# Linear attention and a gated mixture of four attention experts on one core: the work as a task graph with a list scheduler, and squares read from SBUF

## The chip, the core and the metric

The kernel runs on one core of a Trainium2 chip. The core has TensorE for matrix products (PE in the profile; its weight loads are PEld), VectorE (DVE), ScalarE (ACT), GpSimd (POOL), and SyncE (SP), which here only issues DMA transfers. Products land in PSUM, and DVE or ACT copy them from there to SBUF. The metric is the device time of one execution in microseconds (us), as the median of several runs. All inputs and outputs lie in HBM.

## The reference

The numbers are 8 batches, 8 heads, 576 tokens, 64 channels a head, 4 experts. Cut to what matters:

```python
kv = einsum('bhsd,bhse->bhde', k, v)              # 64x64 for each head
out = einsum('bhsd,bhde->bhse', q, kv)
rms = sqrt(mean(out * out, axis=-1) + 1e-06)
x = out / rms * g_norm                            # (8, 576, 512): the 8 heads side by side

logits = x @ w_gate                               # 4 experts, the best 2 kept, softmax of those two
for e in range(4):
    q, k, v = x @ wq[e], x @ wk[e], x @ wv[e]     # 512 -> 64
    scores = causal(scale * (q @ k.T))            # 576x576
    a = exp(scores - scores.max()) / sum
    out += weight_of(e) * (a @ v @ wo[e])         # 64 -> 512
```

## The kernel before

A batch has 576 tokens, which are cut into five blocks (four of 128, one of 64). The work on a batch is three Python generators.

`stage_a` is the linear attention. `kv_pair` multiplies k by v for two heads (80 small matmuls a batch, tile p_kv), and `kv_copy` copies the result twice: DVE into kvx, the operand of the next product, and ACT into a block diagonal tile kv2. `q_block` transposes q on PE (p_q), and DVE copies that to qT. kv2 is transposed (p_kt, kvT) and multiplied by the gate weights (p_kg), which adds four gate columns to each head of kvx. Then each of the five blocks is multiplied by kvx (p_out). DVE copies p_out to o_sb, ACT writes the squares of p_out to sq, and DVE sums sq into ms. When all five are there, a chain of eleven small DVE operations computes one over the root for all tokens (tiles half, u, w, y), and POOL multiplies o_sb by it into x_tok.

`stage_x` transposes x_tok on PE (p_x), and ACT copies it to xT.

`stage_s` is the experts. DVE computes the gates. `v_proj` makes v of all four experts, `proj` makes q and k of one pair of experts (p_proj; ACT copies it to qTp and kT). `scores` makes the scores in five pieces for each pair. A matmul there reads the 64 partitions of one expert of the pair, in kT and in qTp. ACT writes the exponential of each piece to PT, and POOL masks the diagonal. `pv` multiplies by v (p_O), DVE scales by gate over sum (inv, osc), `o_t` transposes (p_OT, OT). `final` multiplies by wo (p_y); ACT copies p_y to y, and SP stores y.

PSUM is two rings. "big" has three slots of two banks (p_out, p_proj, p_sc, p_O), "small" has two slots of one bank (p_kv, p_q, p_kt, p_kg, p_x, p_v, p_OT, p_y).

The order comes from two layers. `merge` interleaves the generators by the costs that they yield, so that in one turn `stage_s` of batch b runs beside `stage_x` of b + 1 and `stage_a` of b + 2. Within `stage_s` a string fixes the order of its parts:

```python
"Q0 Q0 V V S0 V S0 V S0 V S0 Q1 S0 Q1 S1 Y S1 Y S1 P0 P0 P0 S1 P0 P0 S1 Y T0 Y Y P1 P1 P1 P1 P1 T1"
```

The tile layer below then reorders the instructions by its own priorities, and can cut a part in two. Each engine runs its own list in order. Loads are issued by SP in the order in which they are written: batch 0, the weights, batches 1 and 2, then one batch for each turn.

Of the kernel before, what the change touches and what calls it, by code (L numbers as in the profile page):

```python
# [14 lines left out]
AX_X = mybir.AxisListType.X  # L15


@with_exitstack
def kernel(
# [45 lines left out]
    def small(shape, name, dtype=FP32):
        return ps1.tile(shape, dtype, tag="small", name=name)
# [6 lines left out]
    kr, vr, kvx, kv2s, sqs, lg8s, kTs, vexts, mss = [], [], [], [], [], [], [], [], []  # L73
    for j in range(2):
# [16 lines left out]
        nc.gpsimd.memset(t[:], 1.0)  # L91
        vexts.append(t)
        t = const.tile([P, NB, H], FP32, name=f"ms{j}")
        nc.gpsimd.memset(t[REM:P, NF], 1.0)
        mss.append(t)
    ob = const.tile([P, NB, H, GW], FP32, name="o_sb")
    nc.gpsimd.memset(ob[REM:P, NF], 0.0)
    for j in range(3):
        t = const.tile([P, H, Dh + 1], FP32, name=f"sq{j}")
        nc.gpsimd.memset(t[:, :, Dh : Dh + 1], 1e-6)  # L100
        sqs.append(t)
# [36 lines left out]

    loads = {0: load_qkv(0, fine=True)}

    g_wide = const.tile([P, 1], FP32, name="g_wide")
    for r in range(P // Dh):
        nc.sync.dma_start(g_wide[r * Dh : (r + 1) * Dh, :], g_norm.unsqueeze(1))
    wg_st = const.tile([P, NCH, E], FP32, name="wg_st")
    nc.sync.dma_start(wg_st[:], moe_w_gate.rearrange("(c p) e -> p c e", p=P))
    wg_bd = const.tile([P, NCH, 2, E], FP32, name="wg_bd")
    nc.gpsimd.memset(wg_bd[:], 0.0)
    for hh in range(2):
        pp = slice(hh * Dh, (hh + 1) * Dh)
# [3 lines left out]
    w_r = {}
    for name, wdram in (("v", moe_wv), ("q", moe_wq), ("k", moe_wk)):
        wr = const.tile([P, NCH, E, Hd], FP32R, name=f"w{name}_r")
        wf = wst.tile([P, NCH, E, Hd], FP32, name="w_stage", tag="w_stage")
        for e in range(E):
            nc.sync.dma_start(wf[:, :, e, :], wdram[e].rearrange("(c p) f -> p c f", p=P))
        nc.vector.tensor_scalar_mul(
            out=wr[:].rearrange("p c e f -> p (c e f)"),  # L160
            in0=wf[:].rearrange("p c e f -> p (c e f)"),
            scalar1=g_wide[:],
        )
        w_r[name] = wr
    loads[1] = load_qkv(1)
    wo_st = wst.tile([P, EP, D], FP32, name="wo_st", tag="w_stage")
    for pr in range(EP):
        nc.sync.dma_start(
            wo_st[:, pr, :], moe_wo[2 * pr : 2 * pr + 2].rearrange("two d m -> (two d) m")
        )  # L170
    wo_b = const.tile([P, EP, D], BF16, name="wo_b")
    nc.vector.tensor_copy(out=wo_b[:], in_=wo_st[:])

    def kv_pair(p_kv, c, kb, vb, krem, vrem):
# [9 lines left out]
    def kv_copy(p_kv, kvb, kv2):
        for hh in range(2):
            pp = slice(hh * Dh, (hh + 1) * Dh)
            nc.vector.tensor_copy(out=kvb[pp, :, hh, 0:Dh], in_=p_kv[pp, :, :])
            nc.scalar.copy(kv2[pp, :, hh * Dh : (hh + 1) * Dh], p_kv[pp, :, :])  # L188


    def stage_a(b, res):
        qb, kb, vb = loads[b]
        qT = s1.tile([P, NCH, S], FP32, tag="qT", name="qT", bufs=1)
        kvb, kv2 = kvx[b % 2], kv2s[b % 2]

        def q_block(i):
            t0, nt = blocks[i]
            p_q = small([P, NCH, P], "p_q")
            for c in range(NCH):
# [341 lines left out]
    for _ in y_gen:  # L541
        pass
# [30 lines left out]
```

## Time and profile before

| | |
|---|---|
| median of 3 runs | 328.1 us (324.1 to 328.66) |
| the profiled execution's own time | 324.47 us |
| span of its instructions | 322.5 us |
| granted TensorE clock, mean | 0.945 of full speed |
| PE busy | 276.0 us, 86% |
| PEld busy (weight loads) | 220.4 us, 68% |
| DVE busy | 189.2 us, 59% |
| ACT busy | 153.0 us, 47% |
| POOL busy | 79.5 us, 25% |
| chain that ended last | PE 70%, DVE 10%, ACT 9%, SP's queue 4% |

"Busy" of PE is a union of matmuls whose ends are modelled, and matmuls are pipelined: the next starts before the one ahead has drained. So the pace of PE is read from start to start within a group of equal instructions, and not from the length of one. The weight load of a matmul is an instruction of its own, shown on PEld.

### The profile page before, as it was taken

How to read it: one execution, taken by the hardware profiler on the slowest of the kernel's cores; microseconds unless marked ns; L12 is line 12 of the kernel's file. 1: busy time of each engine (PE TensorE's matmuls, PEld its weight loads, DVE VectorE, ACT ScalarE, POOL GpSimd, SP SyncE). 2: the span in 40 equal slices, each digit the busy share in tenths (PEclk: the TensorE clock that was granted, in tenths of full speed). 3: DMA queues.
4: the chain of work that ended last, by engine and by line, in shares of the span. 5: the costliest groups of instructions: out<-in, count | busy, mean ns of one | idle time of the engine just before them, and what ended most of it. 6: DMA issues, size and time to landing. Idle time of an engine off the chain costs nothing.

```text
span 322.5 us, 6704 instructions
## 1 busy us (share of the span) xinstructions
PE 276.0 (86%) x2624; PEld 220.4 (68%) x2624; DVE 189.2 (59%) x537; ACT 153.0 (47%) x273; POOL 79.5 (25%) x148
## 2 busy tenths in 40 slices
PE   1675579799979997999889996999889996999984
PEld 1565468588858775887667875887667875867641
DVE  0249948846884568646775578546774578424130
ACT  0203123653464654545554554545555554585843
POOL 8100600441044110702053101612052101630210
PEclk9959599999999999799999999799999999899977
DMA  6977999999704269194608372001200120021124
GB/s 195 243 199 195 205 301 223 298 180 276 152 2 133 64 202 192 41 253 127 169 3 269 81 182 58 2 0 67 82 2 2 65 83 0 0 100 53 65 83 147
DMA packets 75280, 40.30 MB, mean 125 GB/s; under 512 B 54000, under 2 KB 70384, under 8 KB 75248
## 3 DMA queue, kind: packets, MB, share of 16 engines
q1 hardware_dynamic: 75248, 39.86, 47.1%
q8 instruction: 21, 0.34, 0.5%
q14 instruction: 11, 0.09, 0.1%
HBM read 30.42 MB, written 9.44 MB: 124 GB/s over the span
## 4 chain that ended last, share of the span: by engine, by line
PE 70%; DVE 10%; ACT 9%; SPq 4%; issue 3%; POOL 1%; DMA 1%; DVEq 0%; ACTq 0%; POOLq 0%
PE p_proj L373 11%; PE p_out L242 11%; PE p_v L355 7%; PE p_sc L400 7%; PE p_O L451 7%; PE p_y L506 6%; PE p_q L200 6%; PE p_x L313 6%; PE p_kv L179 5%; ACT PT L410 3%; PE p_kg L224 3%; DVE o_sb L249 3%; SPq L134 2%; PE p_OT L484 2%; POOL x_tok L297 1%
## 5 line engine op out<-in xcount | busy, mean ns | idle before, releaser
L415 POOL TENSOR_SCALAR_AFFINE_SELECT PT<-PT 128x256 bf16<-128x256 bf16 (+1 forms) x80 | 29.3, 381 | 143.4 <-ACT PT L410 143.4
L410 ACT ACTIVATE PT<-p_sc 128x576 bf16<-128x576 f32 (+3 forms) x80 | 53.9, 714 | 20.1 <-PE p_sc L400 18.1
L297 POOL TENSOR_TENSOR x_tok<-o_sb,y 128x512 f32<-128x512 f32 (+1 forms) x40 | 42.0, 1080 | 85.1 <-DVE y L280 85.0
L242 PE MATMUL p_out<-kvx,qT 128*128 128x136 f32 (+1 forms) x320 | 48.1, 292 | 0.0
L400 PE MATMUL p_sc<-qTp,kT 64*128 64x288 f32 (+2 forms) x192 | 35.7, 358 | 10.7 <-ACT PT L410 5.9
L242 PEld LDWEIGHTS p_out<-kvx,qT 128*128 128x128 f32 (+1 forms) x320 | 40.2, 181 | 4.8 <-ACT sq L253 2.1
L253 ACT ACTIVATE sq<-p_out 128x512 f32<-128x512 f32 (+1 forms) x40 | 23.8, 596 | 39.9 <-DVE o_sb L249 38.4
L318 ACT CAST xT<-p_x 128x512 fp32r<-128x512 f32 (+1 forms) x40 | 21.8, 545 | 34.3 <-PE p_x L313 34.3
L400 PEld LDWEIGHTS p_sc<-qTp,kT 64*128 64x128 f32 x192 | 19.8, 185 | 21.9 <-ACT PT L410 8.5
L179 PE MATMUL p_kv<-v_b,k_b 128*64 128x64 f32 x512 | 25.7, 260 | 10.3 <-DMA v_b<-in_v_dram 10.3
L249 DVE COPY o_sb<-p_out 128x544 f32<-128x544 f32 (+1 forms) x40 | 28.7, 719 | 7.7 <-PE p_out L242 7.2
L362 DVE CAST vext<-p_v 128x256 bf16<-128x256 f32 (+1 forms) x40 | 17.0, 425 | 26.3 <-PE p_v L355 25.6
L259 DVE TENSOR_REDUCE ms<-sq 128x8 f32<-128x520 f32 (+1 forms) x40 | 27.4, 688 | 7.9 <-ACT sq L253 7.8
L205 DVE COPY qT<-p_q 128x512 f32<-128x512 f32 (+1 forms) x40 | 24.7, 634 | 11.6 <-PE p_q L200 11.0
L451 PEld LDWEIGHTS <-PT 128*128 128x128 bf16 (+2 forms) x480 | 24.1, 103 | 10.8 <-issue 5.3
L179 PEld LDWEIGHTS p_kv<-v_b,k_b 128*64 128x64 f32 x512 | 23.0, 173 | 12.2 <-DMA k_b<-in_k_dram 6.7
L451 PE MATMUL p_O<-vext,PT 128*128 128x65 bf16 (+2 forms) x480 | 30.3, 199 | 0.4 <-ACT PT L410 0.4
L313 PE MATMUL p_x<-ident_f,x_tok 128*128 128x128 f32 (+1 forms) x160 | 25.9, 289 | 5.4 <-POOL x_tok L297 4.3
L355 PE MATMUL p_v<-wv_r,xT 128*128 128x256 f32 (+1 forms) x160 | 28.3, 300 | 0.7 <-ACT kv L188 0.7
L373 PE MATMUL p_proj<-xT,wk_r 128*128 128x288 f32 x128 | 24.3, 314 | 3.6 <-ACT qTp L384 3.6
L506 PE MATMUL p_y<-wo_b,OT 128*128 128x512 bf16 (+1 forms) x80 | 25.1, 417 | 0.7 <-ACT OT L489 0.7
L511 ACT COPY y<-p_y 128x512 f32<-128x512 f32 (+1 forms) x40 | 23.0, 595 | 5.0 <-PE p_y L506 2.7
(67 smaller groups left out, 360.9 us busy)
## 6 DMA issues: line engine op xcount, KB each, us to landing
q_b<-in_q_dram SPq DMA_DIRECT2D x32, 256.0 KB, 5.2
out_dram<-y SPq DMA_DIRECT2D x32, 256.0 KB, 2.1
k_b<-in_k_dram SPq DMA_DIRECT2D x7, 1024.0 KB, 6.0
v_b<-in_v_dram SPq DMA_DIRECT2D x7, 1024.0 KB, 10.2
k_b<-in_k_dram SPq DMA_DIRECT2D x4, 256.0 KB, 4.7
v_b<-in_v_dram SPq DMA_DIRECT2D x4, 256.0 KB, 4.9
k_rem<-in_k_dram SPq DMA_DIRECT2D x8, 128.0 KB, 9.2
v_rem<-in_v_dram SPq DMA_DIRECT2D x8, 128.0 KB, 7.5
```

What stands on the lines that cost most here:

```text
L179: nc.tensor.matmul(p_kv[hh * Dh : (hh + 1) * Dh, c, :], lhsT=lk, rhs=rv, start=(j == 0), stop=(j == NF), skip_group_check=True,)
L242: nc.tensor.matmul(p_o[:nt, c // 2, (c % 2) * 2 * GW : (c % 2 + 1) * 2 * GW], lhsT=qT[:, c, t0 : t0 + nt], rhs=kvb[:, c, :, :].rearrange(" ...
L249: nc.vector.tensor_copy(out=ob[:nt, i].rearrange("p (k h) g -> p k (h g)", k=2), in_=p_o[:nt, :, 0 : 4 * GW])
L297: nc.gpsimd.tensor_tensor(out=xt[:nt], in0=ob[:nt, i, :, 0:Dh], in1=y[:nt, i * H : (i + 1) * H].unsqueeze(2).to_broadcast([nt, H, Dh]), op ...
L313: nc.tensor.transpose(p_x[:, c, :nt], xts[i][:nt, 2 * c : 2 * c + 2, :].rearrange("p h d -> p (h d)"), ident_f[:nt, :nt],)
L355: nc.tensor.matmul(p_v[:nt, :], lhsT=xT[:, c, t0 : t0 + nt], rhs=w_r["v"][:, c, :, :].rearrange("p e f -> p (e f)"), start=(c == 0), stop= ...
L373: nc.tensor.matmul(p_p[:, s, 0:HALF], lhsT=w_r[nm][:, c, 2 * pr : 2 * pr + 2, :].rearrange("p e f -> p (e f)"), rhs=xT[:, c, s * HALF : (s ...
L400: nc.tensor.matmul(p_s[:, el, o : o + hi - lo], lhsT=kTp[pb, kb * P : (kb + 1) * P], rhs=qTp[pb, lo:hi], start=True, stop=True,)
L410: nc.scalar.activation(PT[:, :, d0 : d0 + o], p_s[:, :, 0:o], ACTF.Exp, scale=scale)
L415: nc.gpsimd.affine_select(out=d, in_=d, compare_op=AluOpType.is_ge, fill=0.0, base=0, pattern=[[0, 2], [1, w]], channel_multiplier=-1,)
L451: nc.tensor.matmul(p_O[:nq, bank, (2 * n + el) * (Hd + 1) : (2 * n + el + 1) * (Hd + 1)], lhsT=PT[:nk, el, col : col + nq], rhs=vx[:nk, kb ...
L506: nc.tensor.matmul(p_y[:nq, :], lhsT=OT[:, pr, s0 : s0 + nq], rhs=wo_b[:, pr, :], start=(pr == 0), stop=(pr == EP - 1),)
```

## The change

The generators, `merge` and the string are gone. `graph` writes each piece of work as a task, with its engine, how long it holds the engine, when its result is there, the tasks that it needs, and the ring slots that it uses. `plan` is a list scheduler that runs when the program is built: again and again it takes the task that can start earliest, and of those of that engine that can start within 0.02 us of it the one of lowest `urgency`, a number for each kind of task from the tables OFFSET and STEP and the batch number. The kernel then emits the tasks in that order, under `manual_schedule`, in which the tile layer doesn't reorder. Tasks of equal urgency (the four parts of a load, blocks of the same q) come in the order in which Python walks a set, which the text doesn't fix: two builds of it stand in different orders at such places.

Beside the order, some operations are others:
- the squares are read from o_sb, so that p_out has one reader, the copy by DVE;
- the ACT copy of p_kv is one instruction for all partitions (kvc), without the block diagonal; p_kt takes two transposes instead of four, p_kg two matmuls instead of four, with gate weights laid out for that;
- kT is now two tiles for each pair, one for each expert, with zeros in the other expert's 64 partitions. A score matmul reads all 128 partitions, and the copy of k is two ACT instructions of 64 partitions;
- k and v come in two transfers each (four in batch 0), the gate weights are loaded first, and the weights wq, wk and wv behind k and v of batch 2.

The sizes of the two rings stay: `"sm": 2, "bg": 3`.

```diff
+    def pe(name, hold, needs, tiles=()):
+        add(name, "PE", hold, hold + 0.27, needs, tiles)
+
+    def act(name, took, needs, tiles=()):
+        add(name, "ACT", took - 0.10, took + 0.06, needs, tiles)
...
+        for c in R4:
+            piece = c if b == 0 else c // 2
+            pe(("kv", b, c), 0.88, [("lk", b, piece), ("lv", b, piece), ("lr", b)], (("sm", "kv", b), ("k", b), ("v", b)))
...
+            pe(("out", b, i), 0.93, [("qc", b, i), ("kvx", b), ("kgc", b)], (("bg", "out", b, i), ("qT", b)))
+            dve(
+                ("oc", b, i), 0.73, [("out", b, i), ("xm", b - 1, i), ("gl", b - 1), ("sq", b - 1, i)],
+                (("bg", "out", b, i),),
+            )
+            n = NB * b + i - 3
+            act(("sq", b, i), 0.60, [("oc", b, i), ("red", n // NB, n % NB)])
...
+    o = n[1] * PERIOD + OFFSET[kind]
+    if kind in STEP:
+        o += n[2] * STEP[kind]
...
+    while len(order) < len(tasks):
+        starts = []
+        for eng, ns in cand.items():
+            f = free[eng]
+            for n in ns:
+                t = ready[n]
+                for tl in tasks[n][4]:
+                    if tl not in held:
+                        t = max(t, min(slots[tl[0]], default=none))
+                if eng == "PE" and t > f - 0.15:
+                    t += 0.1
+                starts.append((max(t, f), prio[n], eng, n))
+        t0, _, eng, _ = min(starts)
+        t, _, _, n = min(((t, p, e, n) for t, p, e, n in starts if e == eng and t <= t0 + 0.02), key=lambda x: x[1])
...
-            sq = sqs[i % 3]
-            nc.scalar.activation(
-                sq[:nt, :, 0:Dh].rearrange("p (k h) d -> p k h d", k=2),
-                p_o[:nt, :, 0 : 4 * GW].rearrange("p k (h g) -> p k h g", g=GW)[:, :, :, 0:Dh],
-                ACTF.Square,
-                scale=1.0 / (Dh**0.5),
-            )
...
+    def sq_act(b, i):
+        nt = blocks[i][1]
+        nc.scalar.activation(
+            sqs[(NB * b + i) % 3][:nt, :, 0:Dh], ob[:nt, i, :, 0:Dh], ACTF.Square, scale=1.0 / (Dh**0.5)
+        )
...
+    def kvc_copy(b):
+        nc.scalar.copy(kvcs[b % 2][:], small(None, "kv", b)[:])
...
+    def k_proj_copy(b, pr):
+        for el in range(2):
+            pb = slice(el * Hd, (el + 1) * Hd)
+            nc.scalar.copy(
+                kTs[pr][el][pb, 0:S].rearrange("p (s n) -> p s n", s=2), big("k", b, pr)[pb, :, 0:HALF]
+            )
...
-                        pb = slice(el * Hd, (el + 1) * Hd)
-                        nc.tensor.matmul(
-                            p_s[:, el, o : o + hi - lo],
-                            lhsT=kTp[pb, kb * P : (kb + 1) * P],
-                            rhs=qTp[pb, lo:hi],
...
+                nc.tensor.matmul(
+                    p_s[:, el, o : o + hi - lo],
+                    lhsT=kTs[pr][el][:, kb * P : (kb + 1) * P],
+                    rhs=tiles["qTp", b, pr][:, lo:hi],
...
+    tasks = graph(B)
+    with tc.manual_schedule():
+        for _, _, n in plan(tasks, POOLS, {n: urgency(n) for n in tasks})[0]:
+            emit[n[0]](*n[1:])
```

The first place is on PE, where the second pair of experts of a batch in the middle gets its scores. Before, the end of the product p_proj for k, the last transposes p_OT of the batch ahead, and the score pieces p_sc stand in a row, and then come p_x and p_kv of other batches:

```order
L373 MATMUL p_proj<-xT,wk_r 128x288 x5
L484 LDWEIGHTS osc
L484 MATMUL p_OT<-ident_b,osc 128x128
L400 MATMUL p_sc<-qTp,kT_132 128x288
L484 LDWEIGHTS osc
L484 MATMUL p_OT<-ident_b,osc 128x64
L400 MATMUL p_sc<-qTp,kT_132 128x288 x3
L400 MATMUL p_sc<-qTp,kT_132 128x448 x2
L400 MATMUL p_sc<-qTp,kT_132 128x320 x2
L313 MATMUL p_x<-ident_f,x_tok 128x128 x4
L179 MATMUL p_kv<-v_b,k_b 64x64 x8
```

Now (p_k and p_q at L633 are the products for k and q, p_q at L433 transposes q of a later batch, kT_118 and kT_121 belong to the two experts):

```order
L633 MATMUL p_k<-xT,wk_r 128x288 x8
L633 MATMUL p_q<-xT,wq_r 128x288 x8
L448 MATMUL p_kt<-ident_f,kvc_80 128x128 x2
L433 MATMUL p_q<-ident_f,q_b 128x128 x4
L458 MATMUL p_kg<-wg_bd,kvT 128x16 x2
L659 MATMUL p_sc<-qTp,kT_118 128x288
L659 MATMUL p_sc<-qTp,kT_121 128x288
L433 MATMUL p_q<-ident_f,q_b 128x128 x4
L659 MATMUL p_sc<-qTp,kT_118 128x288
L659 MATMUL p_sc<-qTp,kT_121 128x288
L433 MATMUL p_q<-ident_f,q_b 128x64 x4
L659 MATMUL p_sc<-qTp,kT_118 128x448
```

Work of a later batch has moved between the product for k and the scores that need its copy, and between one score piece and the next.

The second place is SP's queue at the start. Before, the weights (w_stage) stand between the loads of batch 1:

```order
L134 DMA q_b<-in_q_dram 64x8x64
L143 DMA g_wide<-in_g_norm_dram 64x1 x2
L145 DMA wg_st<-in_moe_w_gate_dram 128x4x4
L158 DMA w_stage<-in_moe_wv_dram 128x4x64 x4
L116 DMA k_b<-in_k_dram 128x8x256
L158 DMA w_stage<-in_moe_wq_dram 128x4x64 x4
L116 DMA v_b<-in_v_dram 128x8x256
L158 DMA w_stage<-in_moe_wk_dram 128x4x64 x4
```

Now k and v of batch 2 are ahead of them:

```order
L369 DMA q_b<-in_q_dram 128x8x64 x4
L369 DMA q_b<-in_q_dram 64x8x64
L352 DMA v_b<-in_v_dram 128x4x256
L352 DMA k_b<-in_k_dram 128x4x256
L352 DMA v_b<-in_v_dram 128x4x256
L365 DMA k_rem_74<-in_k_dram 64x8x64
L365 DMA v_rem_76<-in_v_dram 64x8x64
L352 DMA k_b<-in_k_dram 128x4x256
L392 DMA w_stage<-in_moe_wq_dram 128x4x64 x4
L392 DMA w_stage<-in_moe_wk_dram 128x4x64 x4
```

The weights for q and k have moved behind batch 1 and behind k and v of batch 2.

## Rows read from the trace of the kernel before

**Rows 1.** Stretches: length, busy PE, PEld, DVE, ACT, POOL (instructions), clock, DMA share, GB/s

```profile
0.00:55.50 55.50, 34.75 (x325) 30.14 (x325) 29.74 (x67) 10.37 (x19) 14.07 (x33) 0.85 0.93 223
...
158.70:172.30 13.60, 11.03 (x148) 9.07 (x148) 10.67 (x38) 6.81 (x13) 6.29 (x8) 1.00 0.23 56
172.30:194.20 21.90, 21.52 (x180) 17.20 (x180) 12.67 (x30) 11.97 (x22) 2.51 (x7) 1.00 0.64 183
...
314.00:322.50 8.50, 3.93 (x9) 0.94 (x9) 0.00 (x0) 3.15 (x6) 0.00 (x0) 0.74 0.40 140
```

**Rows 2.** Chain that ended last, in order of time: start, length, what

```profile
55.54 1.26 PE p_proj L373 x8
...
158.69 1.34 PE p_proj L373 x8
...
165.16 2.01 ACT PT L410 x3
...
168.39 0.98 DVE gt L341
...
172.36 0.74 PE p_v L355 x4
...
194.21 1.34 PE p_proj L373 x8
```

**Rows 3.** Waits of PE's weight loads, 158.7 to 194.2 us: total, times, longest

```profile
PEld p_sc L400 <- ACT PT L410: 1.2, 1, 1.2
PEld p_proj L373 <- ACT qTp L384: 1.0, 1, 1.0
PEld p_sc L400 <- ACT kT L384: 1.0, 2, 0.8
PEld L451 <- issue: 0.6, 2, 0.4
...
PEld p_out L242 <- issue: 0.2, 1, 0.2
```

**Rows 4.** Groups of PE and PEld in the timeline (the first from the chain)

```profile
95.41 2.48 PE p_kv L179 x80
...
194.20 1.09 PEld L373 LDWEIGHTS p_proj<-xT,wq_r 128*128 128x128 f32 x8 [0.58 <-ACT sq L253]
196.77 1.08 PEld L451 LDWEIGHTS <-PT 128*128 128x128 bf16 x18
199.69 0.40 PE L400 MATMUL p_sc<-qTp,kT 64*128 64x288 f32 x2 [0.66 <-ACT kT L384]
...
211.77 0.53 PEld L355 LDWEIGHTS p_v<-wv_r,xT 128*128 128x128 f32 x4
...
218.26 1.03 PE L506 MATMUL p_y<-wo_b,OT 128*128 128x512 bf16 x4
...
220.12 0.91 PEld L200 LDWEIGHTS p_q<-ident_f,q_b 128*128 128x128 f32 x8
...
224.44 0.99 PEld L242 LDWEIGHTS p_out<-kvx,qT 128*128 128x128 f32 x8 [0.42 <-ACT sq L253]
```

**Rows 5.** Groups of the whole span: busy, mean ns of one, idle before and releasers

```profile
L253 ACT ACTIVATE sq<-p_out 128x512 f32<-128x512 f32 (+1 forms) x40 | 23.8, 596 | 39.9 <-DVE o_sb L249 38.4 <-DVE inv L468 1.4
...
L400 PE MATMUL p_sc<-qTp,kT 64*128 64x288 f32 (+2 forms) x192 | 35.7, 358 | 10.7 <-ACT PT L410 5.9 <-ACT kT L384 4.7
...
L384 ACT CAST kT<-p_proj 128x576 fp32r<-128x576 f32 x16 | 10.2, 639 | 18.7 <-PE p_proj L373 18.7
```

**Rows 6.** Timeline: how long two small PSUM slots are held, p_kv and p_q

```profile
202.87 1.12 PE L179 MATMUL p_kv<-v_b,k_b 128*64 128x64 f32 x16
...
208.53 0.37 ACT L188 COPY kv<-p_kv 64x256 f32<-64x256 f32 x1 [0.49 <-DVE kvx L187]
...
214.17 0.60 PE L200 MATMUL p_q<-ident_f,q_b 128*128 128x128 f32 x4
...
214.81 0.69 DVE L205 COPY qT<-p_q 128x512 f32<-128x512 f32 x1 [1.01 <-PE p_q L200]
```

More of the change, by code (lines that the diff above doesn't have):

```diff
@@ L90 @@
         t = const.tile([P, NB, E, Hd + 1], BF16, name=f"vext{j}")
-        nc.gpsimd.memset(t[:], 1.0)
+        nc.gpsimd.memset(t[:, :, :, Hd : Hd + 1], 1.0)
         vexts.append(t)
[L93 to L101, printed above, removed]
@@ L153 @@
[L153 to L161, printed above, removed]
+    kTs = []
@@ L162, with lwo @@
             scalar1=g_wide[:],
         )
[L164 to L174, printed above, removed]
+    def lwo(_, pr):
+        t = buf(("y", "wo", pr), [P, D], FP32, "wo_st")
+        nc.sync.dma_start(t[:], moe_wo[2 * pr : 2 * pr + 2].rearrange("two d m -> (two d) m"))
@@ L175, in kv_pair, with wo, kv @@
+    def wo(_, pr):
+        nc.vector.tensor_copy(out=wo_b[:, pr, :], in_=tiles["y", "wo", pr][:])
+    def kv(b, c):
+        p_kv = small([P, NCH, Dh], "kv", b)
         for j in range(NF + 1):
@@ L182, in kv_pair, with kvx_copy @@
                 )
[L184 removed]
+    def kvx_copy(b):
+        p_kv = small(None, "kv", b)
         for hh in range(2):
             pp = slice(hh * Dh, (hh + 1) * Dh)
[L187 to L199, printed above, removed]
[L200 to L223 removed]
@@ new lines, in q_copy, with kt, kt_copy @@
+    def q_copy(b, i):
+        t0, nt = blocks[i]
+        qT = buf(("qT", b), [P, NCH, S], FP32, "qT")
+        nc.vector.tensor_copy(out=qT[:, :, t0 : t0 + nt], in_=small(None, "q", b, i)[:, :, :nt])
+    def kt(b):
+        p_kt = small([P, EP, P], "kt", b)
+        for m in range(EP):
+            nc.tensor.transpose(
+                p_kt[:, m, :], kvcs[b % 2][:, 2 * m : 2 * m + 2, :].rearrange("p c e -> p (c e)"), ident_f[:]
+            )
+    def kt_copy(b):
+        nc.vector.tensor_copy(out=buf(("kvT", b), [P, EP, P], FP32, "kvT")[:], in_=small(None, "kt", b)[:])
@@ new lines, in rd, with gate, v_mm @@
+    def rd(b):
+        nc.vector.reciprocal(small_t(b, "rd", [P, NB]), st["den", b][:])
+    def gate(b):
+        nc.vector.tensor_tensor(
+            out=buf(("gate", b), [P, NB, E], FP32, "gate")[:], in0=st["gt", b][:],
+            in1=st["rd", b][:].unsqueeze(2).to_broadcast([P, NB, E]), op=AluOpType.mult,
+        )
+    def v_mm(b, i):
+        t0, nt = blocks[i]
+        p_v = small([P, E * Hd], "v", b, i)
+        for c in range(NCH):
+            nc.tensor.matmul(
+                p_v[:nt, :],
+                lhsT=tiles["xT", b][:, c, t0 : t0 + nt],
+                rhs=w_r["v"][:, c, :, :].rearrange("p e f -> p (e f)"),
+                start=(c == 0),
+                stop=(c == NCH - 1),
+            )
@@ L502, in final @@
-    def final(b, OT):
-        for qc, (s0, nq) in enumerate(blocks):
-            p_y = small([P, D], "p_y")
-            for pr in range(EP):
-                nc.tensor.matmul(
-                    p_y[:nq, :], lhsT=OT[:, pr, s0 : s0 + nq], rhs=wo_b[:, pr, :],
-                    start=(pr == 0), stop=(pr == EP - 1),
-                )
-            y = ysb.tile([P, D], FP32, tag="y", name="y")
-            nc.scalar.copy(y[:nq, :], p_y[:nq, :])
-            nc.sync.dma_start(out[b, s0 : s0 + nq, :], y[:nq, :])
-            yield 0.45
@@ new lines, in ot_copy, with y_mm, y_copy @@
+    def ot_copy(b, pr):
+        nc.scalar.copy(buf(("OT", b), [P, EP, S], BF16, "OT")[:, pr, :], small(None, "ot", b, pr)[:])
+    def y_mm(b, qc):
+        s0, nq = blocks[qc]
+        p_y = small([P, D], "y", b, qc)
+        for pr in range(EP):
+            nc.tensor.matmul(
+                p_y[:nq, :], lhsT=tiles["OT", b][:, pr, s0 : s0 + nq], rhs=wo_b[:, pr, :],
+                start=(pr == 0), stop=(pr == EP - 1),
+            )
+    def y_copy(b, qc):
+        nq = blocks[qc][1]
+        nc.scalar.copy(buf(("y", b, qc), [P, D], FP32, "y")[:nq, :], small(None, "y", b, qc)[:nq, :])
```

813 lines of the change are left out of this document (471 added, 342 removed).

## Prediction

> **What bounds the kernel now.** I read the stretches first, then the chain, then the waits. The chain starts p_proj for a new pair of experts at 158.69 and again at 194.21 [rows 2]: a batch in the middle takes 35.5 us. The stretches cut that batch in two [rows 1]. In its last 21.9 us PE is busy for 21.52. In its first 13.6 us PE is busy for 11.03 and its weight loads for 9.07, and there the chain leaves PE: ACT's exponentials at 165.16, then the gates on DVE at 168.39, and PE again with p_v at 172.36 [rows 2]. No other engine is near its limit in this batch: DVE is busy for 10.67 + 12.67 = 23.3 us, ACT for 18.8, POOL for 8.8 [rows 1]. So PE's queue sets the time, partly by its own pace and partly by waiting.
>
> How much is pace? I divide groups that run without a wait by their count [rows 4]. p_kv takes 2.48 us for its 80. p_proj: 1.09/8 = 0.136 each, 32 a batch, 4.4. p_O: 1.08/18 = 0.06, 60 a batch, 3.6. p_v: 0.53/4 = 0.13, 20, 2.65. p_y: 1.03 for four, of which I take off 0.2 as drain, 0.21 each, 10, 2.1. p_q: 0.91/8 = 0.114; 16 whole and 4 half ones, 2.1, and p_x the same. p_kt (4) and p_kg (8) at that pace 0.46 and 0.9. p_out: 0.99/8 = 0.124, 40, 4.95. p_OT at the pace of p_O 0.6. The sum is 26.3. The scores come in pairs, one for each expert. Two of 288 columns last 0.40 [rows 4], where one lasts 0.358 on average [rows 5]: the second adds 0.04, though p_proj of the same width needs 0.136 each. A pair is then 0.18, and a batch has 3,200 columns of pairs, as many as 11.1 pairs of 288: 2.0. In all **28.3 us of pace**. The waits of the weight loads in this batch (13 rows, from 1.2 to 0.2) add up to 6.9 us [rows 3]. The remaining 35.5 - 28.3 - 6.9 = 0.3 is small steps.
>
> PE's busy time in the same batch is 11.03 + 21.52 = 32.55 of 35.5 us [rows 1], its weight loads' 26.3. By the first there are 3 us to gain, by the second 9, and the sum of paces is nearer to the second. The Trainium skill (Perfetto Trace Analysis, the section on identifying the most-contended engine) holds matmul busy time to be a bad measure, because matmuls are pipelined, and takes the busy share of weight loads. The rows here bear that out; the other reading is a rival below.
>
> **The change, part by part.**
>
> *Fewer transposes and gate products.* p_kt goes from 4 to 2, p_kg from 8 instructions to 4: 6 x 0.114 = 0.7 us less pace. ACT copies p_kv once instead of twice, 0.37 less [rows 6].
>
> *Scores over 128 partitions.* A pair no longer shares the array, so each matmul is paced like p_proj: 11.1 x 2 x 0.136 = 3.0 instead of 2.0, **1.0 us more a batch**. Bounds: nothing, if the pair before didn't run together and the 0.40 is only modelled ends, and 1.5 (11.1 x 0.136), if the second was free. I take 1.0, from the row of this very operation. The Trainium skill (TensorEngine Tiling, When to Use Tiling) says to split the array by rows when the contraction is 64 deep, for up to twice the rate; this part of the change does the opposite. By that rule the price is the 1.5, which is 12 us over eight batches instead of 8.
>
> *The copy of k in two.* Each half has the same columns, so I price it like the whole, 0.64 [rows 5]: 1.3 us more on ACT a batch, and 0.64 later for the scores. In the new order p_q of the pair, p_kt, p_kg and a transpose stand between p_k and its scores (the first place in the section on the change), about 1.1 + 0.2 + 0.45 + 0.45 = 2.2 us of PE work, which hides it. Without that cover it would cost 2 x 0.64 a batch, 10 us in all.
>
> *Squares from SBUF.* The square waits for the copy of p_out either way: 38.4 of its 39.9 us of idle time ended with that copy [rows 5]. What is gone is its hold on a big PSUM slot, 0.6 us for each block after the copy. PE waited for that: the loads of p_proj and p_out at 194.20 and 224.44 show 0.58 and 0.42 us behind sq [rows 4]. About 1 us a batch, contained in the 6.9. No row shows ACT reading that much from SBUF; anything from 0.1 us less to 0.2 us more an instruction would lie under ACT's idle time of 16 us a batch, so I take nothing. New is that o_sb must not be overwritten before the square has read it, but the copy already waits for POOL and DVE to read the same tile, later than the square.
>
> *The order.* The waits that an engine ended, 5.2 of the 6.9 us, come from short distances: p_proj for k behind the copy of q (1.0), scores behind the copy of k (1.0) and behind the exponential of earlier pieces (1.2) [rows 3]. Before, p_k, the scores and each next piece follow one another. Now 2 us of work of a later batch lie between p_k and the scores, and a transpose between pieces. I take these waits as gone. The five rows of "issue" (1.7 us, 0.6 the largest [rows 3]) no engine ended, and I keep them. A batch is then 28.3 - 0.7 + 1.0 = 28.6 of pace, 0.3 of small steps and 1.7 of issue: **30.6 us**. DVE (23), ACT (18.8 + 1.3 - 0.4 = 19.7) and POOL (9) still fit under that.
>
> *The start.* p_proj first runs at 55.54 [rows 2]; DMA until then moves 223 GB/s at a share of 0.93 [rows 1], so the start is a matter of bytes. The new queue brings batch 0 (3,456 KB), wo (512), batch 1 (3,456), k and v of batch 2 (2,304), then wq and wk (1,024). k and v of batch 2 are there after 9.96 MB, at 45 us, and wk after 11.0 MB, at 49. On PE p_kv of batch 2 stands ahead of most of p_x of batch 0 and three blocks of p_out of batch 1, so these start at 45 at the earliest: 2.5 + 2.1 + 3.0 + 0.7 + 0.5 = 8.8 us, and p_proj starts at 54. I keep 55.5. Moving the weights gains nothing, since batch 2 takes their place, but more is done by then: three p_kv (7.4), p_q (4.7), p_kt and p_kg (2.0), two p_out (9.9), p_x (2.1), 26.1 us of pace.
>
> *The end.* In the last 8.5 us PE has 9 matmuls of p_y [rows 1], 1.9 us at their pace. The last copy, p_y, copy and store have no other batch to fill them: 6 us stay.
>
> **Sum.** Pace left after 55.5 us: 8 x 28.6 - 26.1 = 202.7. Stretched by 30.6/28.6: 216.9. With the start and the end 55.5 + 216.9 + 6 = 278.4 us of span, and 2.0 us outside it (324.47 - 322.5): **280 us**. That is made against the profiled execution, 324.47, which is 3.6 under the median of 328.1; I add nothing for that. The three runs lie within 1.4%, so about 2% is what a measurement of this kernel can tell from no change.
>
> **Rivals.**
>
> *PE's busy time is real.* Then a batch can't go under 32.55 + 0.3 = 32.9 us: 55.5 + 202.7 x 32.9/28.6 + 6 + 2 = 297. The same comes out if half of the 5.2 us comes back as waits at other places, because a plan made of fixed costs meets other ones on the chip (33.2, 299). For it speaks that each engine now keeps its list whatever happens; against it the stretch with 9.07 us of loads in 13.6.
>
> *The order does nothing.* The plan's order holds, but where one wait was another of the same length stands, and the batch stays at 35.5: 55.5 + 202.7 x 35.5/28.6 + 6 + 2 = 315 with what is done ahead, up to 325 without. Part of it would be that the order isn't one order: equal urgencies fall differently in each build. The tasks so exchanged are alike, so I give that 4 us at most, both ways.
>
> *Slower: the two small PSUM slots.* A batch turns them 25 times. p_kv holds one for 6.0 us (202.87 to 208.90), the others for some 1.3 (214.17 to 215.50 for p_q) [rows 6]: (24 x 1.3 + 6)/2 = 19 us a batch. The new order puts squares, copies of y and exponentials of several batches into ACT's one list. If the copy that frees a slot stands behind one other of 0.6 us, that is 26, still under PE's pace. From a turn of 2.9 us, when nearly three stand ahead, the batch takes 38 and the kernel is 2% slower; at 3.0 us it is 39 and the time 55.5 + 202.7 x 39/28.6 + 8 = 340. Against it: PE, DVE and ACT are given their order by one plan that counts these slots.
>
> **How the numbers follow.** The forecast (259 to 290) has 0.60, better than that 0.05 (the pace of the weight loads, 26.3, without any wait, would give about 250), the rival at 297 (290 to 312) 0.20, no effect (312 to 332) 0.08, slower 0.07. The predicted time is 280. The range runs from 256 to 312: it leaves out the slow rival, most of no effect and some of the best case. Faster by over 2% is 0.60 + 0.05 + 0.20 = 0.85; within 2% 0.08; slower 0.07.
>
> **What would show it.** p_proj starts at about 55 and then every 30 to 31 us. PE's waits on the copies of q and k and on the exponentials shrink to under 2 us a batch; no load of PE waits for sq. The scores' matmuls start one after the other instead of in pairs. PE's busy share rises over 90% in the middle. Wrong would be: a batch of over 33 us; PE waits that end with DVE or ACT copies of the small ring (qT, xT, vext, y); a start later than 60 us because the weights come too late.

## The result, and the profile after

The changed kernel takes 285.6 us (285.5 to 285.91), the kernel before in the same comparison 326.1 (323.42 to 328.66). The ratio is 0.878, with an interval of 0.870 to 0.887. The forecast was 280 in a range of 256 to 312, so the direction and the size hold, with 5.6 us more than the sum. The profiled execution took 285.5 us, its span 283.4. In all sets, ratios leave out executions more than 1.5% above a kernel's fastest, while medians and ranges take in all.

I read the stretches first, as in [rows 1]:

```profile
0.00:57.00 57.00, 38.24 (x399) 34.28 (x400) 34.01 (x82) 11.22 (x20) 10.88 (x31) 0.94 0.93 218
57.00:110.00 53.00, 49.24 (x471) 43.15 (x470) 45.52 (x137) 31.40 (x56) 16.79 (x25) 1.00 0.92 224
110.00:140.00 30.00, 28.27 (x307) 25.70 (x305) 17.41 (x44) 18.66 (x34) 7.74 (x17) 0.94 0.60 145
140.00:170.00 30.00, 30.00 (x327) 26.62 (x326) 22.08 (x69) 20.28 (x36) 8.89 (x15) 1.00 0.63 164
170.00:200.00 30.00, 29.05 (x322) 26.02 (x321) 22.16 (x67) 19.71 (x35) 8.93 (x15) 1.00 0.11 38
200.00:230.00 30.00, 30.00 (x327) 26.60 (x326) 22.11 (x70) 20.18 (x36) 8.88 (x15) 1.00 0.13 44
230.00:260.00 30.00, 29.21 (x290) 25.14 (x289) 15.39 (x67) 23.51 (x42) 10.68 (x20) 1.00 0.18 63
260.00:283.40 23.40, 18.29 (x150) 12.05 (x148) 5.96 (x25) 15.04 (x26) 3.75 (x10) 0.92 0.29 102
```

From 140 to 230 us PE is busy for 29.05 to 30.00 of every 30 us, and its weight loads for 26.0 to 26.6. Before, a batch of 35.5 us had a stretch of 13.6 us with 9.07 of loads. That stretch is gone. The ends are less full: 43.15 of 53 us of loads after the start, 12.05 of 23.4 at the end.

The chain, as in [rows 2], gives the pace (p_proj is now p_q and p_k at L633):

```profile
57.03 1.06 PE p_k L633 x8
...
138.66 1.07 PE p_q L633 x8
...
168.13 1.06 PE p_q L633 x8
...
198.51 1.07 PE p_q L633 x8
...
228.01 1.07 PE p_q L633 x8
```

The chain has the first product for k or q at 57.03 (it starts at 56.8), where it was at 55.54. From 138.66 on, the same place of a batch comes after 29.47, 30.38 and 29.50 us: 29.8 on average. In the kernel before, it came at 122.02, 158.69, 194.21, 230.88 and 266.43: batches of 36.7 and 35.5 us in turn, 36.1 on average. Two of them as stretches, with the columns of [rows 1]:

```profile
122.00:158.70 36.70, 34.05 (x329) 27.85 (x329) 23.49 (x67) 18.66 (x34) 8.79 (x15) 0.95 0.63 156
158.70:194.20 35.50, 32.55 (x328) 26.27 (x328) 23.35 (x67) 18.77 (x34) 8.80 (x15) 1.00 0.48 135
```

They differ in the granted clock: in the longer one it was at the lower of its two levels (0.50, which is 1.2 GHz) from 130.5 to 133.5 us, after PE had been busy for only 1.58 of 3 us (127 to 130). In the changed kernel it is 1.00 from 140 to 230 us. So of the 6.3 us that a batch has become shorter, 0.6 goes with the clock. Why it didn't fall in the batch from 158.7 as well, where PE was busy for 1.48 of 3 us (163 to 166), is not shown.

The waits of PE's weight loads from 140 to 230 us (total, times, longest) are all that is left of [rows 3] in three batches:

```profile
PEld p_sc L659 <- issue: 1.2, 3, 0.4
PEld L695 <- issue: 0.9, 1, 0.9
PEld p_q L433 <- issue: 0.7, 3, 0.3
PEld p_kv L415 <- ACT y L754: 0.6, 3, 0.2
PEld L747 <- issue: 0.6, 3, 0.2
```

That is 4.0 us in 90, or 1.3 a batch, and only 0.6 of it ended with an engine. It is the copy of y, which frees a small slot of [rows 6], 0.2 us at a time. Over the whole span, the two waits between ACT and the scores were, in the kernel before,

```profile
PEld p_sc L400 <- ACT PT L410: 8.5, 9, 1.2
...
PEld p_sc L400 <- ACT kT L384: 7.6, 14, 1.0
```

and are now

```profile
PEld p_sc L659 <- ACT PT L673: 1.4, 3, 0.7
...
PEld p_sc L659 <- ACT kT L648: 0.4, 1, 0.4
```

The groups that answer to [rows 5]:

```profile
L659 PE MATMUL p_sc<-qTp,kT 128*128 128x288 f32 (+2 forms) x192 | 39.2, 325 | 0.5 <-ACT PT L673 0.5
...
L494 ACT ACTIVATE sq<-o_sb 128x512 f32<-128x512 f32 (+1 forms) x40 | 25.3, 635 | 21.5 <-DVE o_sb L488 20.1
...
L648 ACT CAST kT<-p_k 64x576 fp32r<-64x576 f32 x32 | 20.3, 635 | 11.1 <-PE p_k L633 10.9
```

A square from SBUF takes 635 ns, where it took 596 from PSUM. Each half of the copy of k takes 635, as long as the whole did (639).

### The profile page after: what moved, and what is told of

Read it like the earlier page. It is cut to its first block, busy times and chain, and to the rows that moved or that the text cites. A ratio compares the mean times of both kernels' runs of the same rounds, so it can differ in the third digit from the quotient of the medians.

```text
span 283.4 us, 6610 instructions
## 1 busy us (share of the span) xinstructions
PE 252.3 (89%) x2576; PEld 219.6 (77%) x2576; DVE 184.7 (65%) x554; ACT 160.0 (56%) x281; POOL 76.5 (27%) x146
## 4 chain that ended last, share of the span: by engine, by line
PE 70%; DVE 14%; DMA 6%; SPq 5%; ACT 2%; issue 2%; ACTq 0%; DVEq 0%
PE p_out L478 12%; PE p_sc L659 9%; PE p_pv L695 7%; PE p_y L747 7%; PE p_k L633 6%; PE p_v L615 6%; PE p_q L633 6%; PE p_q L433 5%; PE p_kv L415 5%; PE p_x L433 4%; SPq L352 3%; DMA w_stage<-in_moe_wq_dram 2%; DMA w_stage<-in_moe_wv_dram 2%; DVE inv L719 2%; DVE mk L588 2%; DVE osc L726 2%
## 5 line engine op out<-in xcount | busy, mean ns | idle before, releaser
L679 POOL TENSOR_SCALAR_AFFINE_SELECT PT<-PT 128x256 bf16<-128x256 bf16 (+1 forms) x80 | 30.1, 387 | 153.1 <-ACT PT L673 139.5
L553 POOL TENSOR_TENSOR x_tok<-o_sb,rs 128x512 f32<-128x512 f32 (+1 forms) x40 | 41.8, 1061 | 40.7 <-DVE rs L529 33.1
L659 PE MATMUL p_sc<-qTp,kT 128*128 128x288 f32 (+2 forms) x192 | 39.2, 325 | 0.5 <-ACT PT L673 0.5
L494 ACT ACTIVATE sq<-o_sb 128x512 f32<-128x512 f32 (+1 forms) x40 | 25.3, 635 | 21.5 <-DVE o_sb L488 20.1
L659 PEld LDWEIGHTS p_sc<-qTp,kT 128*128 128x128 f32 x192 | 28.8, 195 | 5.4 <-issue 1.6
L415 PE MATMUL p_kv<-v_b,k_b 128*64 128x64 f32 x512 | 22.7, 238 | 9.9 <-DMA k_b<-in_k_dram 9.6
L415 PEld LDWEIGHTS p_kv<-v_b,k_b 128*64 128x64 f32 x512 | 19.5, 149 | 12.1 <-DMA v_b<-in_v_dram 9.5
L695 PE MATMUL p_pv<-vext,PT 128*128 128x65 bf16 (+2 forms) x480 | 25.8, 196 | 3.0 <-DVE osc L726 3.0
L695 PEld LDWEIGHTS <-PT 128*128 128x128 bf16 (+2 forms) x480 | 21.5, 101 | 8.8 <-issue 3.1
L433 PE MATMUL p_q<-ident_f,q_b 128*128 128x128 f32 (+1 forms) x160 | 25.7, 291 | 1.5 <-ACT xT L566 1.2
L648 ACT CAST kT<-p_k 64x576 fp32r<-64x576 f32 x32 | 20.3, 635 | 11.1 <-PE p_k L633 10.9
```

The costliest lines, as they stand in the source:

```text
L415: nc.tensor.matmul(p_kv[hh * Dh : (hh + 1) * Dh, c, :], lhsT=lhs, rhs=rhs, start=(j == 0), stop=(j == NF), skip_group_check=True,)
L433: nc.tensor.transpose(p_t[:, c, :nt], src[:nt, 2 * c : 2 * c + 2, :].rearrange("p h d -> p (h d)"), ident_f[:nt, :nt])
L553: nc.gpsimd.tensor_tensor(out=buf(("x", b, i), [P, H, Dh], FP32, "x_tok")[:nt], in0=ob[:nt, i, :, 0:Dh], in1=st["rstd", b][:nt, i * H : (i ...
L659: nc.tensor.matmul(p_s[:, el, o : o + hi - lo], lhsT=kTs[pr][el][:, kb * P : (kb + 1) * P], rhs=tiles["qTp", b, pr][:, lo:hi], start=True, ...
L679: nc.gpsimd.affine_select(out=d, in_=d, compare_op=AluOpType.is_ge, fill=0.0, base=0, pattern=[[0, 2], [1, w]], channel_multiplier=-1,)
L695: nc.tensor.matmul(p_O[:nq, bank, (2 * n + el) * (Hd + 1) : (2 * n + el + 1) * (Hd + 1)], lhsT=PT[:nk, el, col : col + nq], rhs=vexts[b % ...
```

## The experiments

Three sets ran, on three chips, each beside the kernel before (324.9, 328.0 and 327.8 us). Across sets I compare ratios. Unless a diff says otherwise, each kernel from the fifth on is the second one plus its edit. Line numbers differ by up to eight between them.

**Is the order one order?** The first kernel is the same text built once more, with no edit.

> The changed kernel's own text, built once more, so that tasks of equal urgency may stand in another order. My theory (the exchanged tasks are alike): 282 to 290 us, within 4 us of 285.6. Rival (the time hangs on one lucky order): more than 6 us away, above 292 us.

The second fixes the order of equal tasks as the graph lists them, the third in reverse (`-rank[x[3]]`):

```diff
+    rank = {n: i for i, n in enumerate(tasks)}
-        t, _, _, n = min(... if e == eng and t <= t0 + 0.02), key=lambda x: x[1])
+        t, _, _, n = min(... if e == eng and t <= t0 + 0.02), key=lambda x: (x[1], rank[x[3]]))
```

> The changed kernel, with ties of urgency broken by the place of the task in the graph (block 0 first), so that each build is the same. My theory: 282 to 290 us. Rival (the order among equals matters): above 292 or under 279 us.

> The same with ties broken the other way round (block 4 first). My theory: within 4 us of the run with ties in graph order. Rival: more than 6 us from it.

The same text built again takes 287.93 us (286.49 to 291.68; ratio 0.884, 0.876 to 0.893). Ties in the order of the graph give 282.56 (282.06 to 283.08; 0.870, 0.863 to 0.877), ties reversed 293.34 (291.44 to 299.15; 0.901, 0.891 to 0.910). So tasks that look alike are worth 0.031 of the time before, some 10 us, between the two ends. Stretches of the rebuilt kernel,

```profile
57.00:110.00 53.00, 50.33 (x534) 44.15 (x533) 45.45 (x128) 27.44 (x50) 14.05 (x20) 1.00 1.08 250
110.00:140.00 30.00, 28.58 (x242) 23.26 (x242) 23.21 (x76) 22.38 (x40) 11.16 (x18) 1.00 0.39 106
140.00:230.00 90.00, 87.56 (x960) 78.06 (x960) 60.23 (x175) 61.79 (x110) 27.62 (x53) 1.00 0.26 75
```

and of the one with ties in graph order:

```profile
57.00:110.00 53.00, 51.16 (x507) 45.68 (x506) 47.14 (x139) 34.26 (x62) 19.62 (x29) 1.00 0.95 216
110.00:140.00 30.00, 27.95 (x294) 25.27 (x295) 19.77 (x58) 20.06 (x36) 5.22 (x12) 1.00 0.61 158
140.00:230.00 90.00, 89.06 (x988) 79.27 (x986) 66.49 (x205) 60.51 (x107) 26.88 (x46) 1.00 0.30 80
```

Between 57 and 140 us the second gets 70.95 us of weight loads done and the first 67.41, which is 3.5 us more; up to 57 us it was 0.8 behind. In the 90 us after that, the difference is 1.2. Between these two, a tie decides how the first batches run into one another, and little of the middle. Where the reversed order loses its time stays open.

**The squares alone, in the kernel before.** One operand is changed (sq stays, written as one stretch):

```diff
-                sq[:nt, :, 0:Dh].rearrange("p (k h) d -> p k h d", k=2),
-                p_o[:nt, :, 0 : 4 * GW].rearrange("p k (h g) -> p k h g", g=GW)[:, :, :, 0:Dh],
+                sq[:nt, :, 0:Dh],
+                ob[:nt, i, :, 0:Dh],
                 ACTF.Square,
```

> The kernel before with one edit: ACT squares o_sb instead of p_out. My theory (the order is the gain, the early release of the PSUM slot is worth at most the 1 us a batch that PE's loads waited for sq): 318 to 326 us, ratio 0.98 to 1.00. Rival (the PSUM slots were what held PE back, so the squares are the gain): under 310 us.

It takes 334.46 us (330.96 to 337.22; 1.020, 1.009 to 1.031), over the 318 to 326 expected. It isn't faster; whether it is slower by 2% is unclear. Its chain comes to p_proj every 36.8 to 37.7 us (the next times at 209.19 and 246.86):

```profile
135.44 0.81 PE p_proj L373 x6
...
172.28 0.78 PE p_proj L373 x6
```

Much of that goes with the clock. It falls to the lower level in each of these batches, to a mean of 0.95 in the first two, and in the kernel before the batches with 0.95 take 36.7 us. The largest wait of PE's loads is `p_x <- POOL x_tok`, 10.5 us where it was 7.7. The order isn't quite the old one: in each batch of the middle two matmuls of PE stand elsewhere, one exponential on ACT goes ahead of a copy of OT, and POOL makes one mask ahead of the five multiplications for x_tok. So the run doesn't separate the operand from these exchanges. It does show that the squares, with the order that the tile layer makes of them, bring nothing.

**The changed operations, one by one, in the new order.** The scores on 64 partitions again, as before, with one copy of k:

```diff
-        for el in range(2):
-            pb = slice(el * Hd, (el + 1) * Hd)
-            nc.scalar.copy(
-                kTs[pr][el][pb, 0:S].rearrange("p (s n) -> p s n", s=2), big("k", b, pr)[pb, :, 0:HALF]
-            )
+        nc.scalar.copy(
+            kTs[pr][0][:, 0:S].rearrange("p (s n) -> p s n", s=2), big("k", b, pr)[:, :, 0:HALF]
+        )
...
-                    lhsT=kTs[pr][el][:, kb * P : (kb + 1) * P],
-                    rhs=tiles["qTp", b, pr][:, lo:hi],
+                    lhsT=kTs[pr][0][el * Hd : (el + 1) * Hd, kb * P : (kb + 1) * P],
+                    rhs=tiles["qTp", b, pr][el * Hd : (el + 1) * Hd, lo:hi],
```

> Base is the changed kernel with ties in graph order (282.6 us). Here the scores read 64 partitions of one k tile again, two experts side by side in the array, and the copy of k is one ACT instruction; the order stays. My theory (scores over 128 partitions cost 1.0 us of PE pace a batch, 0 to 1.5): 272 to 278 us, and pairs of p_sc start together. Rival (the scores wait for ACT's exponentials at that place, so the pace is hidden): 281 to 285 us.

276.8 us (276.3 to 278.79; 0.850, 0.842 to 0.859), the shortest of all. PE's timeline with full columns (the second kernel):

```profile
182.39 0.78 PE L660 MATMUL p_sc<-qTp,kT 128*128 128x288 f32 x4
183.01 0.60 PE L434 MATMUL p_q<-ident_f,q_b 128*128 128x128 f32 x4
```

and in pairs:

```profile
178.72 0.53 PE L658 MATMUL p_sc<-qTp,kT 64*128 64x288 f32 x4
179.19 0.66 PE L434 MATMUL p_q<-ident_f,q_b 128*128 128x128 f32 x4
```

From the start of the four to the start of what follows it is 0.62 us and 0.47. In the three batches from 140 to 230 us it is, with full columns, 0.62 where p_q follows and 0.53 where p_y does (three times each), and 0.46 or 0.47 in pairs. A batch in the middle, from p_out to p_out, goes from 29.9 us (156.15 to 215.97 for two) to 29.3 (152.89 to 211.48). That is 0.6 a batch, some 5 of the 5.8 us from 282.56 to 276.8.

The squares from PSUM again:

```diff
-            sqs[(NB * b + i) % 3][:nt, :, 0:Dh], ob[:nt, i, :, 0:Dh], ACTF.Square, scale=1.0 / (Dh**0.5)
+            sqs[(NB * b + i) % 3][:nt, :, 0:Dh].rearrange("p (k h) d -> p k h d", k=2),
+            big("out", b, i)[:nt, :, 0 : 4 * GW].rearrange("p k (h g) -> p k h g", g=GW)[:, :, :, 0:Dh],
+            ACTF.Square, scale=1.0 / (Dh**0.5),
```

> Same base and order, but ACT squares p_out in PSUM, so a big slot is held until the square is done. My theory (the slot's hold is worth about 1 us a batch to PE): 286 to 294 us, and PE's loads wait for sq again. Rival (the plan leaves enough slots free, the squares' move is worth nothing): 281 to 284 us.

286.44 us (282.76 to 286.88; 0.875, 0.863 to 0.888), 3.9 above the second kernel's, though the two intervals overlap widely. The trace has waits for sq again:

```profile
PEld p_out L479 <- ACT sq L495: 3.9, 3, 1.6
```

There are three in the whole span. By p_out of batch 2 it is 4.6 us behind (66.3 against 61.7), and after that the middle runs at the same pace (160.8, 190.2, 220.6). But the granted clock is at the lower level there too, from 51 to 64 us (0.50 from 57 to 64, against 1.00 in the second kernel). What share of the 4.6 us is the waits and what share the clock is not shown.

All of the changed operations undone (squares from PSUM, p_kv copied twice and transposed by four, k copied once, scores in pairs), with the new order kept:

> The new order (ties in graph order) with the operations of before: squares from PSUM, scores over 64 partitions with one copy of k, block diagonal kv, four transposes and four gate products. My theory (the order is the whole gain): 280 to 290 us, from 276.8 with row groups, plus some 4 for the squares, plus 0.7 us a batch for p_kt and p_kg. Rival (the changed operations are what lets the order work): over 300 us.

281.25 us (280.59 to 282.93; 0.859, 0.853 to 0.866), against 0.870 (0.863 to 0.877) for the second kernel. What stays of the change is the order, with the way in which loads are cut, staged and queued, and kT in two fixed tiles instead of three in turn. That by itself gives the whole gain. The other edits together add nothing that can be measured: by the ratios the padded scores cost 6 us (0.870 against 0.850), and the squares and the fewer transposes bring 3 (0.850 against the 0.859 here, with intervals that overlap). Its chain:

```profile
150.07 1.05 PE p_k L627 x8
...
210.01 1.05 PE p_k L627 x8
```

Two batches in 59.9 us.

**The order without `manual_schedule`**: the tasks are emitted in the planned order, and the tile layer may reorder them.

```diff
-    with tc.manual_schedule():
-        for _, _, n in plan(tasks, POOLS, {n: urgency(n) for n in tasks})[0]:
-            emit[n[0]](*n[1:])
+    for _, _, n in plan(tasks, POOLS, {n: urgency(n) for n in tasks})[0]:
+        emit[n[0]](*n[1:])
```

> Changed kernel with ties in graph order, tasks emitted in the plan's order, but not under the manual schedule, so the tile layer reorders them as it did before. My theory (each engine's kept order fills PE's waits): 290 to 320 us. Rival (the order of emission is enough): 281 to 286 us.

298.32 us (296.5 to 299.7; 0.910, 0.903 to 0.916). Its chain in the middle:

```profile
163.05 1.25 PE p_q L634 x8
...
223.11 1.25 PE p_q L634 x8
```

Two batches in 60.1 us, 30.0 each, as with the order kept. The loss lies ahead: p_out of batch 4 starts at 139.5, in the second kernel at 125.7. The granted clock differs there, 0.89, 0.90 and 0.94 in the stretches to 57, 110 and 140 us against 0.97, 1.00 and 1.00, so a part of the loss may be the clock's; the runs don't part the two. Emitting the work in the planned order, with the other operations, brings 29.5 us without the manual schedule (327.78 to 298.32). Keeping each engine to it brings some 13 more (0.910 against 0.870 of 327.8), and that in the first 140 us.

**The weights early**: the plan loads them ahead of k and v of batch 2 (`lw=-35.8, ws=-10.8` become `lw=-82.0, ws=-60.0`).

> Same base, but wq, wk and wv are loaded between the q blocks of batch 0, ahead of batch 1. My theory (the start is a matter of bytes, and what comes earlier pushes back something else): 279 to 286 us, with p_k earlier and p_kv of batches 1 and 2 later by some 6 us. Rival (late weights cost the start dearly): under 277 us.

285.48 us (284.15 to 287.34; 0.876, 0.867 to 0.885), no gain. p_kv of batches 1 and 2 starts at 36.2 and 57.0 instead of 31.1 and 41.4: what the weights gain, the data of these batches lose. The first p_k didn't come earlier, as was expected, but at 61.1 instead of 58.6.

**The rings**: `"sm": 2, "bg": 3` become `"sm": 4, "bg": 2`, which fills the same eight banks.

> Same base, but PSUM is split into four small slots and two big ones instead of two and three; the plan makes a new order for it. My theory (the small ring is not what bounds, at 25 turns and 19 to 26 us a batch it is under PE's pace): not faster, 281 to 300 us, since the big ring gets tight. Rival (the two small slots pace the batch): under 277 us.

312.1 us (311.42 to 314.55; 0.959, 0.949 to 0.969), over the 281 to 300 expected. A batch takes 32.4 us, and PE waits for the exponentials again:

```profile
PEld p_sc L660 <- ACT PT L674: 9.0, 18, 1.0
```

Two more small slots don't make up for one big slot less.

**Two plans that should have been better**, both with the scores in pairs. One puts measured durations into the graph: p_kv 0.62 instead of 0.88, the copy of k 0.64 instead of 1.24, p_O 0.55 and 0.83 instead of 0.38 and 0.56, and loads of k and v about 2.4 times as long as planned (1.1 us a unit instead of 0.45).

> The row group version (276.8 us) with the plan's costs set to what the traces show: loads of k and v 1.1 us for 256 KB instead of 0.45, p_kv, p_pv, p_sc and the copy of k; the urgencies stay. My theory (what is lost at the start and the first three batches is lost because the plan believes that loads come twice as fast): 268 to 275 us. Rival (the urgencies fit the old costs, and the bytes at the start decide anyway): 277 us or more.

The other keeps these durations and fits the urgencies to them anew:

```diff
-    lk=-101.2, lv=-101.2, lr=-101.2, lq=-86.0, lg0=-200, wg=-60, lw=-35.8, ws=-10.8, lwo=-85, wo=-30,
-    kv=-61.6, kvx=-60.6, kvc=-60.6, q=-57.9, qc=-75.4, kt=-138.5, ktc=-138.5, kg=-137.5, kgc=-137.5,
...
+    lk=-54.7, lv=-54.7, lr=-54.7, lq=-51.3, lg0=-200, wg=-290.0, lw=-17.4, ws=-241.8, lwo=212.2, wo=-103.3,
+    kv=-60.5, kvx=56.3, kvc=56.3, q=-56.9, qc=-168.1, kt=-543.0, ktc=-543.0, kg=-200.4, kgc=-200.4, out=-46.8,
...
```

> The same with the urgency table fitted anew to these costs. My theory: 262 to 272 us, with the batches in the middle still at 29 us and the gain in the first 110 us. Rival (start and transition are bound by bytes and by the pace of DVE and PE): 275 us or more.

Both missed: 282.9 us (282.06 to 283.11; 0.862, 0.857 to 0.867) and 281.95 (280.88 to 285.71; 0.859, 0.853 to 0.865), against 276.8 (0.850) for the old numbers. The same two stretches of the kernel with the old numbers (276.8 us),

```profile
57.00:110.00 53.00, 50.98 (x509) 44.02 (x510) 46.62 (x143) 32.35 (x60) 19.62 (x29) 1.00 0.93 218
...
140.00:230.00 90.00, 88.03 (x975) 75.69 (x980) 67.28 (x217) 58.00 (x104) 28.97 (x50) 1.00 0.29 83
```

with measured durations,

```profile
57.00:110.00 53.00, 50.63 (x493) 42.69 (x493) 48.16 (x141) 31.83 (x59) 18.00 (x29) 1.00 0.93 221
...
140.00:230.00 90.00, 89.73 (x990) 76.96 (x989) 68.18 (x214) 57.16 (x103) 26.54 (x45) 1.00 0.30 84
```

and with new urgencies:

```profile
57.00:110.00 53.00, 51.18 (x654) 45.70 (x649) 43.05 (x144) 29.24 (x54) 18.74 (x32) 1.00 0.88 210
...
140.00:230.00 90.00, 85.75 (x861) 72.29 (x859) 64.72 (x188) 52.55 (x94) 22.81 (x40) 0.94 0.26 77
```

Measured durations pack the middle tighter (76.96 us of loads instead of 75.69) and the start less (42.69 instead of 44.02). New urgencies do the reverse, 45.70 and 72.29, but in their middle the granted clock is 0.94 (the lower level from 144 to 150.6 and from 208.5 to 212 us), so the 72.29 is not the order's alone. My theory was that the first 110 us lose time because the plan takes loads to be faster than they are. Its forecasts fell, as no plan gave a shorter time. Of the first 110 us themselves it is neither shown nor refuted: with new urgencies 80.9 us of loads are done by then (35.22 up to 57 us, and 45.70), with the old numbers 76.7, and with measured durations alone 75.6.

## Why the prediction was right, step by step

**The bound and the order.** "I take these waits as gone" held. In the middle 0.2 us a batch of waits that an engine ended is left of 5.2, and 1.1 of issue of 1.7. The two together take 29.8 - 1.3 = 28.5 us of pace, which I had summed to 28.6 + 0.3. So the batch came to 29.8, against 30.6. That the order, with its loads, is the cause is shown by two runs: it alone, with the old operations, gives 0.859, and an order that the tile layer may change again gives 0.910 where the kept one gives 0.870. The squares alone, in nearly the old order, give 1.020. The new loads without the new order, and the fewer transposes (0.7 us a batch in the sum), were not tried alone.

**The batch before.** I read one batch, of 35.5 us, as the batch in the middle. The chain's others were 36.7 and 35.5 in turn, and the prediction has no term for the clock, which fell in every second one. The forecast for the new batch doesn't rest on it, but the gain in the middle is 6.3 us a batch and not 5.7, and the rival that the order does nothing would stand some 4 us higher (36.1 in place of 35.5).

**The start.** 57.03 in the chain against 55.5. The weights ahead of batch 2 gain nothing, as the step on bytes said, and the run with early weights shows the trade.

**The step that was mis-sized: everything between the start and the middle, and the end.** I let the rate of the middle run from 55.5 us to 6 us before the end. In the middle, loads fill 79.24 of 90 us, a share of 0.880 (three rows of the stretches above). At this share the 185.3 us of loads behind 57.0 would take 210.5, where the sum had 216.9, so the middle's rate gave back 6.4. The missing share costs 4.0 us from 57 to 110 (53 - 43.15/0.880), 0.8 to 140, 1.4 from 230 to 260 and 9.7 behind that: 15.9, where the sum had 6. With the start, -6.4 + 9.9 + 1.5 = 5.0 us, the span's 283.4 against 278.4. That the sum came so near is in part luck, as errors of 6.4 and 9.9 us point opposite ways. Part of the end is in the chain:

```profile
271.43 1.50 PE p_pv L695 x30
...
273.38 0.56 DVE osc L726
...
275.02 0.65 ACT OT L741
...
276.82 2.87 PE p_y L747 x6
```

I had counted the last copy, p_y and store. The scaling on DVE and the transposes of the last pair are just as bare, from 272.93 to 275.02, and the last p_y ran at the lower clock level (0.51 from 276.3 to 279.7 us): its six take 2.87 us, where the prediction had 0.21 each. What bounds 57 to 130 us stays open. DMA is at a share of 0.92 to 110 us, but no wait of PE there ended with a load of k or v, and the two other plans only moved the loss about.

**Ties.** "4 us at most, both ways" was too little: ratios from 0.870 to 0.901, with the build on record (0.878) in between. The tasks are alike, but which batch's piece comes first isn't neutral at the start.

**Scores over 128 partitions.** 1.0 us a batch was expected and 0.6 came: four matmuls of 288 columns take 0.53 or 0.62 us whole and 0.46 or 0.47 in pairs. So in the agreement of 28.5 with 28.6 one error hides another: some term of the pace was 0.4 too small, and which one is not known. The bound of nothing (the pair before didn't run together) falls. The Trainium skill (TensorEngine Tiling (Array Packing), Theoretical Speedup) has up to twice the rate for such a contraction of 64. The trace agrees in direction, with 1.1 to 1.3 times.

**The copy of k and the squares.** The copy in halves is hidden: `p_sc <- ACT kT` is 0.4 us in the whole span. The square's slot no longer holds PE, but that was worth nothing in the middle of this order; when it is put back, three waits of 3.9 us together show, beside a lower clock at the start. The square itself became 39 ns longer, inside the bounds, and ACT has room.

**Rivals.** *PE's busy time is real* (297): the batch went below its 32.9 us. PE shows 30.00 of 30 us busy after the change, and pairing the scores still took 0.6 us off a batch, so a full PE row is not a full PE. *The order does nothing* (315 to 325) falls with the runs above. *The two small slots* (340): PE waits 0.2 us at a time for the copy of y (the 6.0 us for which p_kv held its slot were measured at the lower clock, 0.55 from 202 to 205.8 us), and four small slots at the cost of a big one give 312.1.

## What to carry to other kernels

Where one engine is the bound and its waits end with short steps elsewhere, putting a later batch's work between producer and consumer can be worth more than trimming the operations: here 46.5 us (327.78 to 281.25) against nothing that can be measured. Fix the order of ties in such a scheduler before comparing anything, and judge a plan on its first batches and its end as well as on its period, since orders with the same period differed by some 13 us here. Changes that come with a new order should each be undone alone: the shortest kernel is the new order with the scores on 64 partitions as they were, 276.8 us.

## What the runs showed of the hardware that was not expected

Tiny DVE operations with two inputs from SBUF can stand still while POOL runs. In the changed kernel's list of one line (duration in ns, least, median and most of eight), a mask of 20 elements a partition takes

```profile
L588 DVE TENSOR_TENSOR mk<-lg,m x8: 166/174/3685, 43.1 to 237.9; 128x20 f32<-128x20 f32 x8
```

and in its timeline the longest of them and what POOL does are

```profile
89.46 1.01 POOL L679 TENSOR_SCALAR_AFFINE_SELECT PT<-PT 128x256 bf16<-128x256 bf16 x3
...
89.83 3.69 DVE L588 TENSOR_TENSOR mk<-lg,m 128x20 f32<-128x20 f32 x1
90.44 3.04 POOL L553 TENSOR_TENSOR x_tok<-o_sb,rs 128x512 f32<-128x512 f32 x3
93.44 0.17 DVE L579 TENSOR_TENSOR sh<-lg,m 128x20 f32<-128x20 f32 x1
```

It ends at 93.52, POOL's last of the group at 93.48, and the next operation of the same shape takes 0.17. The kernel before had a smaller one: gt took 0.98 in its chain [rows 2], beside a run of five such multiplications from 165.11 to 170.32. There it ended at 169.37, inside the run, and an operation of the same shape at 167.25 took 0.17. The Trainium skill (SBUF — State Buffer, Terms) says that the two engines share a pair of ports by a lock that is held for a whole instruction. The rows agree that the DVE operation is held up and not merely slowed; but in the changed kernel it sat through the masks and three multiplications and not one, and what decides how many is not shown. A DVE operation of 0.17 us on the chain can cost over 3 us in this way: here 3.69 once, and 1.05 and 1.73 in other batches.
